# Attention beside a gated MLP on one core: two stages in a hand-set order, scores in 32-row tiles, spatial and output products filled in between

## The chip, the cores and the metric

The kernel runs on one core of one Trainium2 chip. The core has a matrix engine (PE, with weight loads shown as PEld), a vector engine (DVE), a scalar engine (ACT), a general engine (POOL) and a queue engine (SP). Each works through its own instructions in order and waits for the others by semaphores. Matrix products land in PSUM, eight banks of 512 float32 columns on 128 partitions, and are read from there by DVE or ACT. The metric is device microseconds of one execution; lower is better.

## The reference

The input is 2048 tokens of 512 features. One layer norm feeds two branches, and their outputs are added to the input. Branch A is attention with 32 heads of 16 features, in which a token sees itself and the 255 before it. Branch B is a gated MLP: a projection to 2 x 688 features with GELU, a layer norm of the second half, a 2048 x 2048 product over tokens (the spatial product), a gate with the first half, and a product back to 512.

```python
def reference(A_x, A_wqkv, A_wo, B_x, B_w_in, B_w_sp, B_b_sp, B_w_out):
    ...
        scores = jnp.einsum('bhqd,bhkd->bhqk', q, k) * Dh ** (-0.5)
        idx = jnp.arange(S)
        mask = (idx[:, None] - idx[None, :] >= 0) & (idx[:, None] - idx[None, :] < W)
        scores = jnp.where(mask[None, None], scores, -1000000000.0)
        p = _softmax(scores, axis=-1)
        o = jnp.einsum('bhqk,bhkd->bhqd', p, v)
    ...
        z = _gelu(jnp.einsum('bsd,df->bsf', x, w_in))
        z1 = z[..., :Fh].copy()
        z2 = _layernorm(z[..., Fh:], axis=-1)
        g = jnp.einsum('ts,bsf->btf', w_sp, z2) + b_sp[None, :, None]
        return jnp.einsum('bsf,fd->bsd', z1 * g, w_out)
    x = A_x
    xn = _layernorm(x, axis=-1)
    return x + _A_ref(xn, A_wqkv, A_wo) + _B_ref(xn, B_w_in, B_w_sp, B_b_sp, B_w_out)
```

## The kernel before

Tokens are cut into 16 blocks of 128. A start phase loads x, normalizes it (statistics on DVE, an inverse root by 12 small DVE steps for each 4 blocks, L141 to L166), transposes each block on PE (L195) and copies it to xnT on ACT (L198).

Then come 16 steps, one for each block of queries. A step may hold:

- do_z (L206), two blocks in each of the first 8 steps: the projection to 2 x 688 on PE (L214), then GELU by hand. ACT halves the product (L222), DVE makes the argument in three passes (L224 to L229), ACT takes a tanh (L231), DVE finishes (L233, L239) and sums squares (L243).
- do_proj (L270): keys (L275) and queries (L304) by matmuls that move only 128 columns, values (L283) by matmuls that move 512. Queries are made twice, once for the even and once for the odd heads of a pair, with weights whose other half is zero. They are spread over a zeroed tile (qT4, L313 to L317) so that a matmul with all 128 rows picks one pair of heads.
- do_attention (L322): for each of 8 groups of four heads, scores (L341) of two pairs of heads against two or three key blocks, 256 columns each; exp on ACT (L359); triangular masks by DVE (L367, L373) or, in the first 8 steps, one of them by an added matmul (L349); then the product with the values (L382), 17 columns each, the 17th being the sum of the weights. L391 and L393 divide by that sum, and an SP transpose makes oT (L400).
- do_g (L403), from step 8 on: an SP transpose loads a block of w_sp (L406), 32 matmuls make the spatial product (L411), DVE gates it (L417), an SP transpose makes uT (L422).
- do_final (L425): ten matmuls of 512 columns (L432, L438; the last has 48 rows), an add of x by DVE (L443), a store from the ACT queue (L444).

After step 15, eight do_g and do_final are left and run by themselves. All projections and spatial products share one PSUM tile of two banks (gft), scores and outputs have two such tiles (S_t), and the attention result has one (o_t). The order on each engine is made by the framework's scheduler out of the program order and the dependences.

Of the kernel before, what the change touches and what calls it, by code (L numbers as in the profile page):

```python
# [8 lines left out]
P = 128  # L9
BF = mybir.dt.bfloat16  # L10
# [5 lines left out]
D = 512  # L16
H = 32
DH = 16
W = 256
F = 1376  # L20
FH = 688
NQB = S_TOK // P
NDC = D // P
SM_SCALE = DH ** -0.5
GELU_K = 1.5957691216057308
GELU_C = 0.044715
LN_EPS = 1e-5
NG4 = 4
VW = H * 17
UPAD = 768  # L30
NFC = UPAD // P
Z_RANGES = [(0, 512), (512, FH)]
PJ_AHEAD = 1
# [3 lines left out]
def kernel(  # L37
# [18 lines left out]
    eps_t = pers.tile([P, 1], F32, name="eps_t")  # L56
    xnT = pers.tile([P, NDC, S_TOK], BF, name="xnT")
    wq2 = pers.tile([P, NDC, 2, D], BF, name="wq2")
    wk_sb = pers.tile([P, NDC, D], BF, name="wk_sb")
    wv_sb = pers.tile([P, NDC, D], BF, name="wv_sb")  # L60
    wo_sb = pers.tile([P, NDC, D], BF, name="wo_sb")
    w_out_sb = pers.tile([P, NFC, D], BF, name="w_out_sb")
    z1_all = pers.tile([P, NQB, FH], BF, name="z1_all")
    z2n_all = pers.tile([P, NQB, FH], BF, name="z2n_all")
    b_bf = pers.tile([P, NQB], BF, name="b_bf")
    b_all = pers.tile([P, NQB], F32, name="b_all")
    mvx_all = pers.tile([P, NQB, 2], F32, name="mvx_all")
    mv2_all = pers.tile([P, NQB, 2], F32, name="mv2_all")
    rstdx = pers.tile([P, NQB], F32, name="rstdx")
    rstd2 = pers.tile([P, NQB], F32, name="rstd2")  # L70
    sdx = pers.tile([P, NQB], F32, name="sdx")
    sd2 = pers.tile([P, NQB], F32, name="sd2")
    s1_all = pers.tile([P, NQB], F32, name="s1_all")
    s2_all = pers.tile([P, NQB], F32, name="s2_all")
    mean2 = pers.tile([P, NQB], F32, name="mean2")
    var2 = pers.tile([P, NQB], F32, name="var2")
    maskA01 = pers.tile([P, P], BF, name="maskA01")
    maskC01 = pers.tile([P, P], BF, name="maskC01")
    maskAb = pers.tile([P, 2, P], BF, name="maskAb")
    NQRING = 2  # L80
    qT4s = [pers.tile([P, NG4, 4 * 256], BF, name=f"qT4_{i}") for i in range(NQRING)]

    ps_s = ctx.enter_context(tc.tile_pool(name="ps_s", bufs=2, space=bass.MemoryType.PSUM))
    ps_gf = ctx.enter_context(tc.tile_pool(name="ps_gf", bufs=1, space=bass.MemoryType.PSUM))
    ps_o = ctx.enter_context(tc.tile_pool(name="ps_o", bufs=1, space=bass.MemoryType.PSUM))
    xsp = ctx.enter_context(tc.tile_pool(name="xsp", bufs=4))
    bsm = ctx.enter_context(tc.tile_pool(name="bsm", bufs=6))

    XG = 2
    nc.vector.memset(eps_t[:], LN_EPS)  # L90

    make_identity(nc, ident[:])
    nc.vector.memset(maskA01[:], 1.0)
    nc.gpsimd.affine_select(
        out=maskA01[:], in_=maskA01[:], pattern=[[1, P]], compare_op=ALU.is_ge,
        fill=0.0, base=0, channel_multiplier=-1,
    )
    nc.vector.memset(maskAb[:], 0.0)
    nc.gpsimd.affine_select(
        out=maskAb[:], in_=maskAb[:], pattern=[[0, 2], [1, P]], compare_op=ALU.is_ge,  # L100
        fill=-30000.0, base=0, channel_multiplier=-1,
    )
    nc.vector.memset(maskC01[:], 1.0)
    nc.gpsimd.affine_select(
        out=maskC01[:], in_=maskC01[:], pattern=[[-1, P]], compare_op=ALU.is_gt,
        fill=0.0, base=0, channel_multiplier=1,
    )
    nc.vector.memset(wq2[:], 0.0)
    for i in range(NQRING):
        nc.gpsimd.memset(qT4s[i][:], 0.0)  # L110
    nc.gpsimd.dma_start(out=wo_sb[:], in_=A_wo.rearrange("(c p) n -> p c n", p=P))
    nc.gpsimd.dma_start(
        out=w_out_sb[:, 0:5, :], in_=B_w_out[0:640, :].rearrange("(c p) n -> p c n", p=P)
    )
    nc.gpsimd.dma_start(out=w_out_sb[0:48, 5, :], in_=B_w_out[640:688, :])

    with tc.tile_pool(name="wraw_pool", bufs=1) as wrp:
        w_raw = wrp.tile([P, NDC, 3 * D], BF, name="w_raw")
        nc.sync.dma_start(out=w_raw[:], in_=A_wqkv.rearrange("(c p) f -> p c f", p=P))
        for c in range(NDC):  # L120
            sv = w_raw[:, c, 0:D].rearrange("p (G s e j) -> p G s e j", G=NG4, s=4, e=2, j=DH)
            for e in range(2):
                dv = wq2[:, c, e, :].rearrange("p (G s e j) -> p G s e j", G=NG4, s=4, e=2, j=DH)
                nc.vector.tensor_copy(out=dv[:, :, :, e, :], in_=sv[:, :, :, e, :])
            nc.vector.tensor_copy(out=wk_sb[:, c, :], in_=w_raw[:, c, D : 2 * D])
            nc.scalar.copy(out=wv_sb[:, c, :], in_=w_raw[:, c, 2 * D : 3 * D])

    qpool = ctx.enter_context(tc.tile_pool(name="qpool", bufs=2))
    kring = ctx.enter_context(tc.tile_pool(name="kring", bufs=4))
    vring = ctx.enter_context(tc.tile_pool(name="vring", bufs=4))  # L130
    ep = ctx.enter_context(tc.tile_pool(name="ep", bufs=3))
    lpool = ctx.enter_context(tc.tile_pool(name="lpool", bufs=2))
    otpool = ctx.enter_context(tc.tile_pool(name="otpool", bufs=17))
    cpool = ctx.enter_context(tc.tile_pool(name="cpool", bufs=2))
    wsp_pool = ctx.enter_context(tc.tile_pool(name="wsp_pool", bufs=2))

    with ExitStack() as lctx:
        lt = lctx.enter_context(tc.tile_pool(name="lt", bufs=2))
        RS_G = 4

        def rsqrt_batch(n0):  # L141
            sl = slice(n0, n0 + RS_G)
            vpe = bsm.tile([P, RS_G], F32, name="vpe")
            nc.vector.tensor_scalar(
                out=vpe[:], in0=mvx_all[:, sl, 1], scalar1=LN_EPS, scalar2=None, op0=ALU.add
            )
            hx = bsm.tile([P, RS_G], F32, name="hx")
            nc.vector.tensor_scalar(out=hx[:], in0=vpe[:], scalar1=0.5, scalar2=None, op0=ALU.mult)
            yi = bsm.tile([P, RS_G], mybir.dt.int32, name="yi")
            nc.vector.tensor_scalar(  # L150
                out=yi[:], in0=vpe[:].bitcast(mybir.dt.int32), scalar1=1, scalar2=None,
                op0=ALU.arith_shift_right,
            )
            nc.vector.tensor_scalar(
                out=yi[:], in0=yi[:], scalar1=-1, scalar2=0x5F375A86, op0=ALU.mult, op1=ALU.add
            )
            y = yi[:].bitcast(F32)
            ty = bsm.tile([P, RS_G], F32, name="ty")
            for _ in range(3):
                nc.vector.tensor_tensor(out=ty[:], in0=y, in1=y, op=ALU.mult)  # L160
                nc.vector.tensor_tensor(out=ty[:], in0=ty[:], in1=hx[:], op=ALU.mult)
                nc.vector.tensor_scalar(
                    out=ty[:], in0=ty[:], scalar1=-1.0, scalar2=1.5, op0=ALU.mult, op1=ALU.add
                )
                nc.vector.tensor_tensor(out=y, in0=y, in1=ty[:], op=ALU.mult)  # L165
            nc.vector.tensor_copy(out=rstdx[:, sl], in_=y)  # L166

        xs_tiles = {}
        for n in range(NQB):
            tn = n * P  # L170
            if n % RS_G == 0:
                for n2 in range(n // XG, (n + RS_G) // XG):
                    xs = xsp.tile([P, XG, D], BF, name="xs")
                    eng = nc.sync if n2 % 2 == 0 else nc.scalar
                    eng.dma_start(
                        out=xs[:],
                        in_=x2[n2 * XG * P : (n2 + 1) * XG * P, :].rearrange(
                            "(j p) d -> p j d", p=P
                        ),
                    )  # L180
                    for j in range(XG):
                        nn = n2 * XG + j
                        xs_tiles[nn] = xs[:, j, :]
                        stats = bsm.tile([P, nc.vector.BN_STATS_DIM], F32, name="stats")
                        nc.vector.bn_stats(out=stats[:], in_=xs[:, j, :])
                        nc.vector.bn_aggr(out=mvx_all[:, nn, :], in_=stats[:])
                rsqrt_batch(n)
            xn_sb = lt.tile([P, D], BF, name="xn_sb")
            nc.vector.tensor_scalar(  # L189
                out=xn_sb[:], in0=xs_tiles[n], scalar1=mvx_all[:, n, 0:1],  # L190
                scalar2=rstdx[:, n : n + 1], op0=ALU.subtract, op1=ALU.mult,
            )
            tp = ps_s.tile([P, NDC, P], BF, name="tp", tag="S_t")
            for c in range(NDC):
# [253 lines left out]
    for n in range(PJ_AHEAD):  # L448
        do_proj(n)
# [62 lines left out]
```

## Time and profile before

| what | value |
|---|---|
| median of 3 runs | 442.18 us (440.03 to 445.08) |
| the profiled execution, its span | 445.4 us |
| DMA traffic | 24.77 MB, mean 56 GB/s |
| start phase | about 0 to 45 us |
| steps 0 to 7 | about 45 to 218 us |
| steps 8 to 15 | about 218 to 380 us |
| what is left of do_g and do_final | about 380 to 445 us |

"Busy" counts an instruction from its start to its modelled end. PE's instructions overlap, so a group of matmuls costs the time from one start to the next (the pitch), which is less than the duration of one. The chain is followed back from the last instruction to what released each; time on it is time that the span is made of. The granted clock is PE's, 1.00 being full speed.

### The profile page before, as it was taken

How to read it: one execution, taken by the hardware profiler on the slowest of the kernel's cores; microseconds unless marked ns; L12 is line 12 of the kernel's file. 1: busy time of each engine (PE TensorE's matmuls, PEld its weight loads, DVE VectorE, ACT ScalarE, POOL GpSimd, SP SyncE). 2: the span in 40 equal slices, each digit the busy share in tenths (PEclk: the TensorE clock that was granted, in tenths of full speed). 3: DMA queues.
4: the chain of work that ended last, by engine and by line, in shares of the span. 5: the costliest groups of instructions: out<-in, count | busy, mean ns of one | idle time of the engine just before them, and what ended most of it. 6: DMA issues, size and time to landing. Idle time of an engine off the chain costs nothing. (4 is left out here: it accounts for less than half of the span.)

```text
span 445.4 us, 9799 instructions
## 1 busy us (share of the span) xinstructions
PE 373.5 (84%) x4112; PEld 253.2 (57%) x4112; DVE 284.8 (64%) x682; ACT 240.8 (54%) x344; POOL 25.2 (6%) x62
## 2 busy tenths in 40 slices
PE   0126678899998989898799989898989899999996
PEld 0114355667675757676576656665666667455552
DVE  4919488887979797979965665656565654412222
ACT  3112565696878787979665728374645559100000
POOL 9100000000000000000000000000000000011010
PEclk9975999999999999999989999999999999999999
DMA  8990300000001000000003050604040323566551
GB/s 242 114 179 24 128 1 13 1 13 1 13 1 14 2 13 1 13 8 7 1 13 79 1 102 1 102 1 102 4 100 17 87 38 66 118 161 146 121 130 42
DMA packets 63548, 24.77 MB, mean 56 GB/s; under 512 B 57568, under 2 KB 61664, under 8 KB 63504
## 3 DMA queue, kind: packets, MB, share of 16 engines
q1 hardware_dynamic: 58464, 16.26, 19.7%
q10 hardware_dynamic: 3920, 4.56, 3.3%
q0 software_dynamic: 1120, 3.33, 3.3%
q8 instruction: 32, 0.52, 0.5%
q14 instruction: 12, 0.10, 0.1%
HBM read 8.41 MB, written 2.10 MB: 24 GB/s over the span
## 5 line engine op out<-in xcount | busy, mean ns | idle before, releaser
L359 ACT ACTIVATE E_t<-S_t 128x768 bf16<-128x768 f32 (+2 forms) x256 | 183.9, 769 | 83.5 <-PE S_t L341 47.6
L411 PE MATMUL gft<-z2n_all,wspT 128*128 128x512 bf16 (+1 forms) x512 | 93.9, 309 | 2.4 <-DVE qtmp L313 2.3
L341 PEld LDWEIGHTS <-kT 128*128 128x128 bf16 x720 | 64.1, 97 | 42.9 <-issue 27.8
L341 PE MATMUL S_t<-qT_0_83,kT 128*128 128x256 bf16 x352 | 59.4, 273 | 9.7 <-ACT E_t L359 6.2
L341 PE MATMUL S_t<-qT_1_84,kT 128*128 128x256 bf16 x368 | 60.1, 271 | 8.6 <-ACT E_t L359 7.2
L382 PEld LDWEIGHTS <-E_t 128*128 128x128 bf16 x1440 | 48.5, 96 | 29.5 <-DVE E_t L373 15.0
L382 PE MATMUL o_t<-v_t,E_t 128*128 128x17 bf16 x1440 | 56.8, 171 | 5.0 <-ACT E_t L359 2.8
L411 PEld LDWEIGHTS <-wspT 128*128 128x128 bf16 x512 | 45.3, 97 | 22.6 <-issue 2.0
L367 DVE TENSOR_TENSOR E_t<-E_t,maskA_80 128x512 bf16<-128x512 bf16 x64 | 27.2, 425 | 44.4 <-ACT E_t L359 44.1
L373 DVE TENSOR_TENSOR E_t<-E_t,maskC_81 128x512 bf16<-128x512 bf16 x112 | 46.5, 419 | 12.5 <-ACT E_t L359 12.3
L214 PE MATMUL gft<-w_in_sb,xnT 128*128 128x512 bf16 (+1 forms) x256 | 45.7, 308 | 6.3 <-DMA w_in_sb<-in_B_w_in_dram 2.1
L304 PEld LDWEIGHTS <-wq_61 128*128 128x128 bf16 x512 | 31.7, 102 | 11.7 <-DVE v_t L295 5.9
L304 PE MATMUL gft<-xnT,wq_61 128*128 128x128 bf16 x512 | 34.1, 226 | 4.4 <-DVE yi L165 3.8
L417 DVE SCALAR_TENSOR_TENSOR u_sb<-gft,b_all,z_all 128x688 bf16<-128x688 f32 x16 | 14.2, 890 | 33.1 <-PE gft L411 29.0
L349 PE MATMUL S_t<-maskAb,ident 128*128 128x256 bf16 x128 | 33.8, 272 | 0.0
L214 PEld LDWEIGHTS <-xnT 128*128 128x128 bf16 x256 | 22.3, 97 | 19.5 <-issue 8.5
L195 PE MATMUL tp<-ident,xn_sb 128*128 128x128 bf16 x64 | 8.4, 285 | 29.7 <-DVE xn_sb L189 29.2
L222 ACT ACTIVATE zb<-gft 128x688 bf16<-128x688 f32 x32 | 23.8, 745 | 13.1 <-PE gft L214 11.1
L231 ACT ACTIVATE th<-wt 128x688 bf16<-128x688 bf16 x32 | 24.8, 776 | 6.4 <-DVE wt L229 5.2
L438 PE MATMUL S_t<-w_out_sb,uT 128*128 128x512 bf16 x96 | 25.2, 380 | 0.7 <-DMA uT<-u_sb 0.7
L313 DVE CAST qtmp<-gft 128x1024 bf16<-128x1024 f32 x16 | 19.6, 1223 | 7.5 <-PE gft L304 7.4
L195 PEld LDWEIGHTS <-xn_sb 128*128 128x128 bf16 x64 | 6.3, 130 | 31.2 <-DVE xn_sb L189 30.2
(71 smaller groups left out, 349.1 us busy)
## 6 DMA issues: line engine op xcount, KB each, us to landing
x_ch<-in_A_x_dram POOLq DMA_DIRECT2D x16, 128.0 KB, 3.3
out_dram<-out_sb ACTq DMA_DIRECT2D x16, 128.0 KB, 2.4
w_raw<-in_A_wqkv_dram SPq DMA_DIRECT2D x1, 1536.0 KB, 7.9
w_in_sb<-in_B_w_in_dram ACTq DMA_DIRECT2D x1, 1376.0 KB, 5.8
xs<-in_A_x_dram ACTq DMA_DIRECT2D x4, 256.0 KB, 6.9
xs<-in_A_x_dram SPq DMA_DIRECT2D x4, 256.0 KB, 6.7
w_out_sb<-in_B_w_out_dram POOLq DMA_DIRECT2D x1, 640.0 KB, 16.2
wo_sb<-in_A_wo_dram POOLq DMA_DIRECT2D x1, 512.0 KB, 6.6
```

The lines of the kernel that those rows point to most:

```text
L214: nc.tensor.matmul(zp[:, lo:hi], lhsT=xnT[:, c, tn : tn + P], rhs=w_in_sb[:, c, f0 + lo : f0 + hi], start=(c == 0), stop=(c == NDC - 1),)
L222: nc.scalar.mul(out=zb[:], in_=zp[:, 0:FH], mul=0.5)
L231: nc.scalar.activation(out=th[:], in_=wt[:], func=ACT.Tanh, scale=GELU_K)
L304: nc.tensor.matmul(qpf[:, col0 : col0 + P], lhsT=wq2[:, c, e, G * P : (G + 1) * P], rhs=xnT[:, c, tn : tn + P], start=(c == 0), stop=(c == ...
L341: nc.tensor.matmul(S_tiles[sp][:, 256 * b : 256 * b + 256], lhsT=kTb[:, G, :], rhs=qT[:, G, 256 * s : 256 * s + 256], start=True, stop=not ...
L349: nc.tensor.matmul(S_tiles[sp][:, 512:768], lhsT=ident[:], rhs=maskAb[:].rearrange("p e c -> p (e c)"), start=False, stop=True,)
L359: nc.scalar.activation(out=dste[:, :, b_lo:3, :], in_=src[:, :, b_lo:3, :], func=ACT.Exp, scale=SM_SCALE,)
L367: nc.vector.tensor_tensor(out=regA, in0=regA, in1=maskA01[:].unsqueeze(1).to_broadcast([P, 4, P]), op=ALU.mult,)
L373: nc.vector.tensor_tensor(out=regC, in0=regC, in1=maskC01[:].unsqueeze(1).to_broadcast([P, 4, P]), op=ALU.mult,)
L382: nc.tensor.matmul(o_t[:, bank, 17 * hh : 17 * hh + 17], lhsT=E_t[:, j, 128 * b : 128 * b + 128], rhs=v_tiles[kb][:, 17 * h : 17 * h + 17] ...
L411: nc.tensor.matmul(gf[:, lo:hi], lhsT=wspT[:, c, :], rhs=z2n_all[:, c, lo:hi], start=(c == 0), stop=(c == NQB - 1),)
L438: nc.tensor.matmul(fo, lhsT=uT[0:K, ch, :], rhs=w_out_sb[0:K, ch, :], start=False, stop=(ch == NFC - 1),)
```

## The change

The whole body is rewritten, and the order on each engine is now the order in which the program is written.

Stage 1 makes everything that comes from xnT. x is loaded in seven pieces on the queues of SP and ACT with the weights of do_z in between; the weights of the outputs move from POOL's queue to SP's, behind x. The inverse root is one power on POOL. z_half makes half a projection block and applies GELU in a single ACT instruction; the second layer norm uses bn_stats. qkv_unit makes queries or keys for 128 features and 512 tokens by four matmuls of 512 columns, or values of a block of 128 tokens by four of 512. Queries are made once and copied twice with a mask for even and odd heads (one copy on DVE, one on ACT). 39 of the 48 such units run between the halves of blocks 3 to 15.

Stage 2 is 184 sets. A set takes two pairs of heads, in two row tiles of 32 rows, against 1024 columns of scores in all, followed by one exp of 1024 columns (kinds BC, AB, CA: which key block meets which of two query blocks; 512 columns for one kind in the first two blocks). After the scores of a set come the masks that are due on DVE (one set late), up to 9 matmuls with the values (three sets late), and filler: the 9 units left, spatial products in two halves of 344 columns, and outputs, 1447 columns a set. What is left of the filler runs at the end. PSUM is cut anew: two tiles of two banks for scores, two of one bank for attention results, two of one bank for filler. The store of the result moves from ACT's queue to POOL's.

```diff
+    ctx.enter_context(tc.manual_schedule())
...
     ps_s = ctx.enter_context(tc.tile_pool(name="ps_s", bufs=2, space=bass.MemoryType.PSUM))
+    ps_o = ctx.enter_context(tc.tile_pool(name="ps_o", bufs=2, space=bass.MemoryType.PSUM))
+    ps_f = ctx.enter_context(tc.tile_pool(name="ps_f", bufs=2, space=bass.MemoryType.PSUM))
...
+    def qkv_unit(b, i):
+        t0 = b * 512
+        pt = bank()
+        if i < 8:
+            G, isk = divmod(i, 2)
+            w0 = isk * D + G * P
+            for c in range(NC):
+                nc.tensor.matmul(
+                    pt[:], lhsT=wqkv[:, c, w0 : w0 + P], rhs=xnT[:, c, t0 : t0 + 512],
+                    start=(c == 0), stop=(c == NC - 1),
+                )
+                yield 512
+            if isk:
+                nc.scalar.copy(out=kT[:, G, t0 : t0 + 512], in_=pt[:])
+            else:
+                nc.vector.tensor_scalar(
+                    out=qpad[:, G, 0, t0 : t0 + 512], in0=pt[:],
+                    scalar1=hmask[:, 0:1], scalar2=None, op0=ALU.mult,
+                )
+                nc.scalar.mul(out=qpad[:, G, 1, t0 : t0 + 512], in_=pt[:], mul=hmask[:, 1:2])
...
+        load_x(nc.sync, 0, 1)
+        load_x(nc.scalar, 1, 2)
+        load_x(nc.sync, 2, 3)
+        load_x(nc.scalar, 3, 4)
+        nc.sync.dma_start(out=w_in_sb[:, :, 0:FH], in_=w_in_v[:, :, 0:FH])
+        nc.scalar.dma_start(out=w_in_sb[:, :, FH:F], in_=w_in_v[:, :, FH:F])
+        load_x(nc.sync, 4, 8)
+        nc.sync.dma_start(out=wqkv[:], in_=A_wqkv.rearrange("(c p) f -> p c f", p=P))
+        load_x(nc.sync, 8, 12)
+        load_x(nc.sync, 12, 16)
...
+            nc.gpsimd.tensor_tensor(
+                out=rs[:, 0:k], in0=ve[:, 0:k], in1=mhalf[:, 0:k], op=ALU.pow
+            )
...
+        def z_half(n, half):
+            zp = ps_s.tile([P, 2, 512], F32, name="zp", tag="S")
+            for c in range(NC):
+                for j in range(2):
+                    f0 = half * FH + j * HALF
+                    nc.tensor.matmul(
+                        zp[:, j, 0:HALF],
+                        lhsT=xnT[:, c, n * P : (n + 1) * P],
+                        rhs=w_in_sb[:, c, f0 : f0 + HALF],
+                        start=(c == 0), stop=(c == NC - 1),
+                    )
+            dst = (z1 if half == 0 else z2n)[:, n, :]
+            nc.scalar.activation(
+                out=dst.rearrange("p (j f) -> p j f", j=2),
+                in_=zp[:, :, 0:HALF], func=ACT.Gelu_apprx_tanh,
+            )
...
+            z_half(n, 0)
...
+            if n >= 3:
+                for _ in qkv_unit(*qkv_list.pop(0)):
+                    pass
+            z_half(n, 1)
...
+    def g_unit(t):
+        u = cp.tile([P, UPAD], BF, name="u")
...
+        uT = cp.tile([P, NFC, P], BF, name="uT", bufs=4)
+        nc.sync.dma_start_transpose(out=uT[:], in_=u[:])
+        uTs[t] = uT
+        u_ready[t] = clock[0] + DMA_STEPS
+        if t + 2 < NB:
+            load_wsp(t + 2)
...
+        def pick(self, drain):
+            if self.qkv:
+                return qkv_unit(*self.qkv.pop(0))
+            if self.fq:
+                t = self.fq[0]
+                if t in u_ready and t in o_ready and (
+                    drain or clock[0] >= max(u_ready[t], o_ready[t])
+                ):
+                    self.fq.pop(0)
+                    return f_unit(t)
+            if self.gq:
+                return g_unit(self.gq.pop(0))
+            return None
...
+    def do_scores(J, G, kind, sp):
...
+        for kb, qs, nq, col in segs:
+            for i in range(2):
+                s = 2 * sp + i
+                nc.tensor.matmul(
+                    S[:, i, col : col + 2 * nq],
+                    lhsT=kT[32 * s : 32 * s + 32, G, kb * P : (kb + 1) * P],
+                    rhs=qpad[32 * s : 32 * s + 32, G, :, qs : qs + nq],
+                    start=True, stop=True,
+                )
+        nc.scalar.activation(
+            out=Et[:, 2 * sp : 2 * sp + 2, c0:512], in_=S[:, :, c0:512],
+            func=ACT.Exp, scale=SM_SCALE,
+        )
...
+    PV_RATE = 9
+    total_fill = 9 * 2048 + NB * 32 * HALF + (NB - 2) * (NC + NFC) * 512
+    per_set = total_fill / len(sets)
+    i = 0
+    while i < len(sets) or mask_q or pv_q or pv_cur is not None:
+        clock[0] = i
+        if i < len(sets):
+            J, G, kind, sp, last = sets[i]
+            do_scores(J, G, kind, sp)
+        while mask_q and mask_q[0][0] <= i:
+            do_masks(*mask_q.pop(0)[1])
+        if i < len(sets):
+            if sp == 1:
+                mask_q.append((i + 1, (J, G, kind)))
+            if last:
+                pv_q.append((i + 3, (J, G)))
+        n = 0
+        while n < PV_RATE:
+            if pv_cur is None:
+                if not pv_q or pv_q[0][0] > i:
+                    break
+                pv_cur = pv_unit(*pv_q.pop(0)[1])
+            if next(pv_cur, 0):
+                n += 1
+            else:
+                pv_cur = None
+        if i < len(sets):
+            fill.pull(per_set)
+        i += 1
+    while fill.step(True):
+        pass
```

More of the change, by code (lines that the diff above doesn't have):

```diff
@@ L72 @@
[L72 to L81, printed above, removed]
@@ L94 @@
[L94 to L107, printed above, removed]
@@ L108 @@
[L108 to L126, printed above, removed]
@@ L154, in rsqrt_batch, with z_apply @@
+        def z_apply(n, rs):
             nc.vector.tensor_scalar(
[L155 to L165 removed]
@@ L166, in rsqrt_batch @@
[L166 to L191, printed above, removed]
-            )
-            tp = ps_s.tile([P, NDC, P], BF, name="tp", tag="S_t")
-            for c in range(NDC):
-                nc.tensor.transpose(
-                    out=tp[:, c, :], in_=xn_sb[:, c * P : (c + 1) * P], identity=ident[:]
-                )
-            nc.scalar.copy(out=xnT[:, :, tn : tn + P], in_=tp[:, :, :])
@@ L425, in do_final @@
[L425 to L435 removed]
+                out=z2n[:, n, :], in0=z2n[:, n, :],
+                scalar1=zmv[n // 2][:, n % 2, 0:1], scalar2=rs[:, n % 2 : n % 2 + 1],
```

654 lines of the change are left out of this document (331 added, 323 removed).

## The prediction, on record before the result

> **What bounds the kernel now.** I read the page's busy shares first, then busy time in four stretches (windows), then the chain of waits, and last single runs of instructions in the timeline, for pitches.
>
> ```profile
> PE 373.5 (84%) x4112; PEld 253.2 (57%) x4112; DVE 284.8 (64%) x682; ACT 240.8 (54%) x344; POOL 25.2 (6%) x62
> ...
> 0.00:45.00 45.00, 11.71 (x95) 9.57 (x96) 27.84 (x134) 9.65 (x17) 12.54 (x22) 0.81 0.77 138
> 45.00:218.00 173.00, 150.03 (x1817) 108.06 (x1815) 142.48 (x313) 133.97 (x199) 1.18 (x5) 1.00 0.06 15
> 218.00:380.00 162.00, 150.73 (x1839) 104.57 (x1839) 98.43 (x216) 97.22 (x130) 6.04 (x20) 0.99 0.25 49
> 380.00:446.00 66.00, 61.00 (x367) 30.97 (x364) 16.02 (x22) 0.00 (x0) 5.45 (x15) 0.99 0.52 121
> ```
>
> In each window row the columns are the stretch, its length, busy PE, PEld, DVE, ACT and POOL, the granted clock and the DMA figures. PE is the busiest engine everywhere except in the first 45 us, where it does almost nothing. Busy says how many instructions are in flight, not what they cost, so I price PE by pitch. These rows give it:
>
> ```profile
> 44.71 0.23 PE L195 MATMUL tp<-ident,xn_sb 128*128 128x128 bf16 x1
> ...
> 45.00 0.39 PE L195 MATMUL tp<-ident,xn_sb 128*128 128x128 bf16 x4
> ...
> 265.39 0.45 PE L382 MATMUL o_t<-v_t,E_t 128*128 128x17 bf16 x12
> 265.70 0.71 PE L341 MATMUL S_t<-qT_0_83,kT 128*128 128x256 bf16 x5
> ...
> L341 PE MATMUL S_t<-qT_0_83,kT 128*128 128x256 bf16 x352 | 59.4, 273 | 9.7 <-ACT E_t L359 6.2
> L382 PEld LDWEIGHTS <-E_t 128*128 128x128 bf16 x1440 | 48.5, 96 | 29.5 <-DVE E_t L373 15.0
> L382 PE MATMUL o_t<-v_t,E_t 128*128 128x17 bf16 x1440 | 56.8, 171 | 5.0 <-ACT E_t L359 2.8
> ...
> 260.13 1.00 PE gft L275 x16
> 261.13 0.86 PE gft L283 x4
> 263.77 1.80 PE gft L304 x32
> 265.59 1.24 DVE qtmp L313
> 281.29 1.00 PE gft L275 x16
> 389.22 4.77 PE gft L411 x32
> 393.99 0.86 PE S_t L432 x4
> 394.86 1.40 PE S_t L438 x6
> 396.25 4.77 PE gft L411 x32
> ```
>
> A run lasts (n-1) pitches and one duration. 17 columns: (0.45 - 0.171)/11 = 0.025 us. 256 columns: (0.71 - 0.273)/4 = 0.11. On the chain the runs follow each other, so 512 columns cost 0.86/4 = 0.215, and 128 columns 1.80/32 = 0.056 (a transpose is as cheap: four in 0.39, one lasting 0.23). The 32 matmuls of L411 cost 4.77, of which 0.10 is the way out of the 48-row matmul (below): 4.67/16 = 0.292 for 688 columns, 0.146 for 344.
>
> PE's necessary work by these pitches: transposes 64 x 0.056 = 3.6; do_z 128 pairs x 0.292 = 37.4; do_proj 16 x 3.66 = 58.6; scores 720 x 0.11 = 79; mask matmuls (L349) 128 x 0.11 = 14; values 1440 x 0.025 = 36; spatial 16 x 4.67 = 74.7; outputs 16 x (2.26 + 0.10) = 37.8. Sum 341 of 445.4 us. So 104 us are lost. Where: about 40 in the start phase; some 3 in each step (from one L275 row to the next 21.16 us pass, and the work in it is 3.66 + 48 x 0.11 + 96 x 0.025 + 4.77 + 2.26 = 18.4), of which 1.24 is PE waiting for DVE to empty the only gft tile; the rest while do_z shares that tile with do_proj; and 6 us at the end. From 45 to 218 us DVE is busy 142 of 173 us too, so removing PE work alone would help little there.
>
> **The change part by part.**
>
> Start. x comes in pieces of 128 KB ahead of the big weights. The nearest rows:
>
> ```profile
> x_ch<-in_A_x_dram POOLq DMA_DIRECT2D x16, 128.0 KB, 3.3
> w_in_sb<-in_B_w_in_dram ACTq DMA_DIRECT2D x1, 1376.0 KB, 5.8
> ...
> 40.07 1.89 PE L304 MATMUL gft<-xnT,wq_61 128*128 128x128 bf16 x16 [3.81 <-DVE yi L165]
> ...
> L185 DVE BATCH_NORM_STATS2 stats<-xs 128x6 f32<-128x512 bf16 x16 | 10.5, 670 | 9.4 <-DMA xs<-in_A_x_dram 9.4
> ```
>
> Issue at 0.8, landing 3.3 later, four statistics at 0.67 with their aggregation, the root, one normalization, four transposes and a copy: the first z matmul at about 9 us; w_in, issued behind x (5.8 from issue to landing before), should be there by then. Ends: 8 and 14. At 40 us 16 matmuls of 128 columns took 1.89, a pitch of 0.11 for 0.056: PE starts at half speed. I add 3 us for that.
>
> Stage 1 empties PSUM with instructions like these:
>
> ```profile
> L222 ACT ACTIVATE zb<-gft 128x688 bf16<-128x688 f32 x32 | 23.8, 745 | 13.1 <-PE gft L214 11.1 <-PE S_t L349 1.3 <-DVE z_all L233 0.2
> L198 ACT COPY xnT<-tp 128x512 bf16<-128x512 bf16 x16 | 8.9, 587 | 27.9 <-PE tp L195 27.9
> L393 DVE TENSOR_TENSOR o_norm<-o_t,rsum 128x512 bf16<-128x512 f32 x16 | 10.9, 680 | 0.1
> ```
>
> On PE stage 1 has transposes 3.6, z 32 x 8 x 0.146 = 37.4, 39 units of four 512-column matmuls at 0.86 = 33.5; sum 74.5. All 48 units cost 41.3 against do_proj's 58.6: the zero half of the queries is no longer streamed. GELU by hand goes (six long instructions a half, of which ACT and DVE did 32 each), and one ACT instruction of the size of L222 stays. What is left for ACT is 32 x 0.75 + 16 x 0.59 + 26 x 0.59 = 49 us and for DVE about 62 (statistics like L185, 26 evacuations like L393, normalizations), both under 74.5, so they lie beside PE. Their waits do not all: in a fixed order, a transpose that wants a PSUM tile waits until an evacuation of 0.7 us is through its queue. I take 5 us for that (ends 0 and 15).
>
> The power on POOL replaces 12 small DVE steps a batch; no row shows it. Beyond the start it has a block's time to run, so I take nothing.
>
> Between the stages: a table load and the first exp, 2 us.
>
> Stage 2. Its new element is a matmul with 32 rows. The nearest thing in this trace is the last matmul of do_final, with 48 rows, between neighbours with 128:
>
> ```profile
> 395.56 0.38 PE L438 MATMUL S_t<-w_out_sb,uT 128*128 128x512 bf16 x1
> 395.87 0.39 PE L438 MATMUL S_t<-w_out_sb,uT 48*128 48x512 bf16 x1
> 396.19 0.39 PE L411 MATMUL gft<-z2n_all,wspT 128*128 128x512 bf16 x1
> ```
>
> The starts are 0.31 and 0.32 apart instead of 0.215: 0.10 us to go in, 0.10 to come out, though both sides were ready. Every set has scores with 32 rows and then values and filler with 128, so I charge each set 0.20. Ends: nothing (a 32-row tile may be prepared while the array works), and 0.52. For the upper end, a matmul that lasts 0.38 is followed after 0.215, so 0.165 of it is draining; a switch that waits for all of it and then for a weight load of 0.096 (PEld L382, above) costs 0.26. I take the row itself.
>
> Beside this stands a rule. The Trainium skill, "TensorEngine Tiling (Array Packing)", section "Key Properties", says that changing the tiling mode drains the engine. The 48-row rows agree in kind. By a full drain the sum below would be 59 us longer; the rows show less than half of it.
>
> Scores: two row tiles work on different heads, each 512 columns a set. If they run at the same time, 0.215 a set, and I add 0.03 for the second one's weights (a pitch of 0.025 in L382 is a weight load and a matmul): 0.25. If one waits for the other, 0.43. No run here shows two tiles at once. The Trainium skill, "TensorE: Matmul & The Clock Gate", "Part 3: Packing small matmuls", says tiles in different row groups run concurrently and gives 3.07 times for four; by that two would be near what I take.
>
> Values: 1440 matmuls over 184 sets, 7.83 x 0.025 = 0.20. Filler: 9 units 7.8, spatial 74.7, 14 outputs of 2.36 = 33.0 (their 48-row switch included); 115.5/184 = 0.63. A set costs PE 0.25 + 0.20 + 0.20 + 0.63 = 1.28, and 184 sets 235 us.
>
> Does another engine need more?
>
> ```profile
> 266.39 3.69 ACT L359 ACTIVATE E_t<-S_t 128x768 bf16<-128x768 f32 x5 [2.24 <-PE S_t L341]
> ...
> L359 ACT ACTIVATE E_t<-S_t 128x768 bf16<-128x768 f32 x224 | 169.4, 810 | 78.2 <-PE S_t L341 47.6 <-PE S_t L349 13.2 <-issue 10.4
> L373 DVE TENSOR_TENSOR E_t<-E_t,maskC_81 128x512 bf16<-128x512 bf16 x112 | 46.5, 419 | 12.5 <-ACT E_t L359 12.3
> L224 DVE TENSOR_TENSOR wt<-zb 128x688 bf16<-128x688 bf16 x32 | 16.5, 515 | 10.4 <-ACT zb L222 10.2
> L417 DVE SCALAR_TENSOR_TENSOR u_sb<-gft,b_all,z_all 128x688 bf16<-128x688 f32 x16 | 14.2, 890 | 33.1 <-PE gft L411 29.0 <-issue 4.1
> L391 DVE RECIPROCAL rsum<-o_t 128x32 f32<-128x32 f32 x16 | 5.7, 355 | 6.8 <-PE o_t L382 6.8
> L359 ACT ACTIVATE E_t<-S_t 128x512 bf16<-128x512 f32 x16 | 8.8, 594 | 2.8 <-PE S_t L349 2.7
> ```
>
> Five exps of 768 columns took 3.69, a pitch of 0.72; 0.84 ns a column (810 against 594 for 256 less) makes 0.94 for 1024. That is under 1.28 and hides; were a set cheaper than 0.94 on PE, ACT would hold it at 173 us. Masks: 0.55 ns a column from 419 and 515 gives 0.70 for 1024 and 1.26 for 2048 columns, 80 us in all; with gating 17 (32 halves of L417 at 0.53), 16 output adds of L393's size 11, and 32 norms of about 0.96 (L391, and L393's 0.68 in two pieces of 0.30), DVE has 139 of 235. A mask is done about 0.9 us before its value matmuls come up; that slack is also what the queues may eat. On POOL the store now stands before the next x_ch, and waits for DVE's add; x_ch lands 3.3 after its issue while an output takes 3.5 sets, so an add may wait half a microsecond, with masks behind it, inside the slack. The output weights now stand behind x on SP's queue; their first user comes 30 sets into stage 2. On SP each uT transpose waits for its gate, with the next w_sp load behind it, and both have some 7 sets.
>
> PE still meets unfinished work at times. Before, 2.8 of 21.16 us a step was lost, 13%, with one tile where there are now two; I take 4% or 9.4 us (ends 0 and 31).
>
> Tail. A transpose by SP takes:
>
> ```profile
> oT<-o_norm SPq DMA_TRANSPOSE x16, 3.1
> out_dram<-out_sb ACTq DMA_DIRECT2D x16, 128.0 KB, 2.4
> ```
>
> After the last scores come exp, the largest mask, 48 value matmuls, norm, this transpose, 14 output matmuls, the add and the store: 1.6 past the last set, then 1.2, 1.2, 3.1, 3.2, 0.7 and 3.5 us (2.4 and its issue by POOL); together 14.5 (ends 11 and 18).
>
> Sum: 9 + 3 + 74.5 + 5 + 2 + 235 + 9.4 + 14.5 = 352 us of span. The profiled span of before, 445.4, stands to its median, 442.18, as 1 to 0.993; so 350 us. PE's work falls only from 341 to 314 (queries 17 less, mask matmuls 14 less, scores 33 less, switches 37 more); the other 65 us are waiting that goes.
>
> **The rivals.**
>
> The tiles do not overlap: the row tiling then does not do what it says, since the columns streamed are the same as before. 0.18 x 184 = 33 us more, 384. For: nothing here shows overlap. Against: different rows and different banks.
>
> The switch drains in full: 0.32 x 184 = 59 more, 409. Against: three rows with 0.10.
>
> The switch hides: 0.20 x 184 = 37 less, 313. For: weights of 32 rows might load early. Against: both directions show it.
>
> The hand-set order loses as much as the steps before, 13% of 235 = 31 instead of 9: 372. For: PE takes no other ready work. Against: double tiles.
>
> Slower than before: the round trip of a set is far dearer with 32 rows than with 48. It would need 0.20 + 92/184 = 0.70 us a set to reach 442. Against: that is three and a half times what the 48-row rows show.
>
> **How the numbers follow.** The forecast, 350 with its own range 335 to 366, gets 0.50; no overlap 0.15; order losses 0.12; hidden switch 0.10; full drain 0.08; the dear switch 0.04; 0.01 for the rest. 315 to 392 holds the first three and about half of the hidden switch, 0.82. Changes under 1% can't be told from none. Faster by over 1% holds all but the dear switch and the rest: 0.95; within 1% 0.01; slower 0.04.
>
> **What would show it.** Score matmuls of a pair starting within 0.05 us: overlap; 0.2 apart: none. The first scores and the first value matmul of a set each 0.1 late: the switch. First z matmul near 9 us, stage 2 starting near 94, a set pitch near 1.3, PE busy to the last set, and a tail of about 15. Wrong would be a set pitch above 1.5, long waits of PE for exp or masks, or ACT without gaps.

## The result, and the profile after

The changed kernel takes 337.85 us (median of 4 runs, 337.48 to 338.79) against 443.63 us for the kernel before beside it: a ratio of 0.764, interval 0.760 to 0.769. The forecast was 350 us.

Below are the page's busy shares and the head of its chain, below them the same head and the first piece of the chain for the kernel before, then busy time by stage (the columns as in the prediction: stretch and length, PE, PEld, DVE, ACT, POOL, granted clock, DMA). The stages are cut at the first z matmul, the first and the last scores.

```profile
PE 312.3 (93%) x3079; PEld 154.9 (46%) x3104; DVE 195.6 (58%) x397; ACT 236.4 (70%) x267; POOL 34.5 (10%) x76
...
PE 88%; DMA 3%; DVE 3%; ACT 2%; issue 2%; POOL 0%; SPq 0%; POOLq 0%; ACTq 0%
```

```profile
PE 38%; issue 2%; DVE 2%; ACT 1%; DMA 1%; ACTq 0%; DVEq 0%; SPq 0%
...
244.86 2.02 issue
```

```profile
0.00:8.95 8.95, 1.03 (x8) 0.82 (x9) 5.33 (x16) 2.17 (x4) 3.04 (x9) 1.00 0.81 273
8.95:88.72 79.77, 76.95 (x461) 44.54 (x470) 55.49 (x132) 45.75 (x73) 11.38 (x19) 1.00 0.23 63
88.72:318.00 229.28, 225.92 (x2522) 105.62 (x2537) 130.21 (x240) 187.48 (x190) 17.41 (x44) 1.00 0.36 71
318.00:335.80 17.80, 8.40 (x94) 3.93 (x91) 4.61 (x10) 1.02 (x1) 2.71 (x5) 0.78 0.20 55
```

The chain is now 88% PE. The 38% of before can't be set against it: that chain could be followed back only to 244.86 us, and its shares add up to less than half of the span. What compares is PE's busy share, 84% before and 93% now. In stage 2 ACT has 187 and DVE 130 of 229 us: both have room, and PE has none. What PE does in a set shows in the timeline (start, length, engine, line, operation):

```profile
200.62 0.31 PE L348 MATMUL gf<-z2n,wspT 128*128 128x344 bf16 x1
200.86 0.39 PE L460 MATMUL S<-qpad,kT 32*128 32x512 bf16 x2
201.18 0.38 PE L503 MATMUL o<-v_all,E 128*128 128x17 bf16 x9
201.42 0.74 PE L348 MATMUL gf<-z2n,wspT 128*128 128x344 bf16 x4
202.10 0.39 PE L460 MATMUL S<-qpad,kT 32*128 32x512 bf16 x2
```

Two score matmuls of 512 columns are over in 0.39 us, the duration of one: they start 3 to 4 ns apart, so the row tiles overlap fully. From the last 344-column matmul to the first score 0.24 us pass in place of 0.145, and from the scores to the values 0.32 in place of 0.215. That is the switch, 0.10 in and 0.10 out, as at the 48-row matmul of before. One set takes 201.18 - 200.86 = 0.32, then 0.24 for nine value matmuls and 0.68 for four filler matmuls with the way in: 1.24 us.

### The profile page after: what moved, and what is told of

The parts are those of the page before. It is cut to its first block, busy times and chain, and to the rows that moved or that the text cites. A ratio compares the mean times of both kernels' runs of the same rounds, so it can differ in the third digit from the quotient of the medians.

```text
span 335.8 us, 7241 instructions
## 1 busy us (share of the span) xinstructions
PE 312.3 (93%) x3079; PEld 154.9 (46%) x3104; DVE 195.6 (58%) x397; ACT 236.4 (70%) x267; POOL 34.5 (10%) x76
## 4 chain that ended last, share of the span: by engine, by line
PE 88%; DMA 3%; DVE 3%; ACT 2%; issue 2%; POOL 0%; SPq 0%; POOLq 0%; ACTq 0%
PE gf L348 23%; PE S L460 17%; PE o L503 15%; PE zp L234 11%; PE fo L374 6%; PE fo L380 4%; PE pj_f L93 4%; PE pj_o L93 4%; DMA w_in_sb<-in_B_w_in_dram 2%; PE pj_o L109 2%; PE pj_f L109 2%; DVE qpad L101 1%; ACT qpad L105 1%; DMA oT<-on_4384 1%; ACT E L467 1%
## 5 line engine op out<-in xcount | busy, mean ns | idle before, releaser
L467 ACT ACTIVATE E<-S 128x1024 bf16<-128x1024 f32 (+1 forms) x184 | 184.5, 1007 | 40.8 <-PE S L460 38.6
L348 PE MATMUL gf<-z2n,wspT 128*128 128x344 bf16 x512 | 95.2, 308 | 0.0
L460 PE MATMUL S<-qpad,kT 32*128 32x512 bf16 (+1 forms) x480 | 70.7, 329 | 2.4 <-ACT E L467 2.2
L503 PEld LDWEIGHTS <-E 128*128 128x128 bf16 x1440 | 47.7, 96 | 39.5 <-issue 32.2
L503 PE MATMUL o<-v_all,E 128*128 128x17 bf16 x1440 | 64.0, 172 | 1.7 <-DVE E L483 1.6
L483 DVE TENSOR_TENSOR E<-E,maskCA 128x2048 bf16<-128x2048 bf16 (+1 forms) x32 | 37.0, 1157 | 33.2 <-ACT E L467 33.2
L234 PE MATMUL zp<-w_in_sb,xnT 128*128 128x344 bf16 x256 | 43.9, 319 | 0.3 <-DMA w_in_sb<-in_B_w_in_dram 0.3
L483 DVE TENSOR_TENSOR E<-E,maskA 128x1024 bf16<-128x1024 bf16 x32 | 22.1, 690 | 32.7 <-ACT E L467 32.7
L374 PE MATMUL fo<-w_out_sb,uT 128*128 128x512 bf16 (+1 forms) x81 | 26.9, 392 | 1.0 <-issue 0.2
L483 DVE TENSOR_TENSOR E<-E,maskC 128x1024 bf16<-128x1024 bf16 x28 | 19.3, 689 | 3.8 <-ACT E L467 1.7
```

What stands on the lines that cost most here:

```text
L234: nc.tensor.matmul(zp[:, j, 0:HALF], lhsT=xnT[:, c, n * P : (n + 1) * P], rhs=w_in_sb[:, c, f0 : f0 + HALF], start=(c == 0), stop=(c == NC ...
L348: nc.tensor.matmul(gf[:, 0:HALF], lhsT=wspT[t][:, c, :], rhs=z2n[:, c, j * HALF : (j + 1) * HALF], start=(c == 0), stop=(c == NB - 1),)
L374: nc.tensor.matmul(fo[:], lhsT=uTs[t][0:K, ch, :], rhs=w_out_sb[0:K, ch, :], start=(ch == 0), stop=False,)
L460: nc.tensor.matmul(S[:, i, col : col + 2 * nq], lhsT=kT[32 * s : 32 * s + 32, G, kb * P : (kb + 1) * P], rhs=qpad[32 * s : 32 * s + 32, G, ...
L467: nc.scalar.activation(out=Et[:, 2 * sp : 2 * sp + 2, c0:512], in_=S[:, :, c0:512], func=ACT.Exp, scale=SM_SCALE,)
L483: nc.vector.tensor_tensor(out=ap, in0=ap, in1=m.unsqueeze(1).to_broadcast([P, ap.shape[1], ap.shape[2]]), op=ALU.mult,)
```

## The experiments

Each is a change of the changed kernel, except where it says so. Times are medians in us.

**One row tile.** Both score matmuls of a set read the rows of the first head pair.

```diff
-                s = 2 * sp + i
+                s = 2 * sp
```

> Both score matmuls of a set use the rows of the first head pair, so the second head pair's scores are not computed; columns, exps and everything else stay. In the changed kernel the two start 2 to 4 ns apart. Theory (PE sets the pace of a set, and the two row tiles overlap): they now follow each other, 0.215 us more in each of 184 sets (half of that in 8 of them), so 337.9 + 39 = 377 us. Rival (ACT's exp of 0.92 to 1.02 us sets the pace, and score time hides beside it): 338 to 342 us.

Measured: 375.5. In its timeline:

```profile
200.04 0.74 PE L348 MATMUL gf<-z2n,wspT 128*128 128x344 bf16 x4
200.72 0.60 PE L460 MATMUL S<-qpad,kT 32*128 32x512 bf16 x2
201.25 0.38 PE L503 MATMUL o<-v_all,E 128*128 128x17 bf16 x9
```

The pair now takes 0.60 instead of 0.39, and 184 x 0.21 is the 38 us. So the overlap is worth 38 us, and PE, not ACT, sets the pace of a set.

**Scores apart.** One row tile before the values, the other behind them.

```diff
+            do_scores(J, G, kind, sp, 0)
...
+            do_scores(J, G, kind, sp, 1)
             fill.pull(per_set)
```

> The two row tiles of a set are issued apart: one before the matmuls with the values, one behind them, so a set goes into the 32-row matmuls and out of them twice; everything is computed as in the changed kernel. Theory (0.2 us for each round trip, and the overlap of the two tiles lost, which by the run with one row tile is worth 37.7 us): 337.9 + 37.7 + about 175 sets with values x 0.2 = 410 us. Rival (the round trip costs nothing of its own, only the loss of overlap counts): 376 us.

Measured: 408.6, 33 us over the run with one row tile: 0.19 us for each of some 175 more round trips. Its timeline:

```profile
201.09 0.38 PE L463 MATMUL S<-qpad,kT 32*128 32x512 bf16 x1
201.40 0.39 PE L508 MATMUL o<-v_all,E 128*128 128x17 bf16 x9
201.72 0.39 PE L463 MATMUL S<-qpad,kT 32*128 32x512 bf16 x1
202.04 0.76 PE L348 MATMUL gf<-z2n,wspT 128*128 128x344 bf16 x4
```

Scores to values, values to scores and scores to filler are each 0.31 to 0.32 apart, where 512 columns cost 0.215 and nine value matmuls 0.24 without a switch behind them. The switch is paid in full in the kernel's time, and does not hide.

**48 rows padded to 128.** Zeros in the output weights.

```diff
+        nc.gpsimd.memset(w_out_sb[:, 5, :], 0.0)
...
-            K = P if ch < NFC - 1 else FH - (NFC - 1) * P
+            K = P
```

> The last 48 rows of the output weights are padded with zeros to 128, so that the 48-row matmul of each output has 128 rows; the columns streamed are the same. Theory (0.10 us in and 0.10 out for each change of the row tiling): 16 x 0.2 = 3.2 us less, 334.7 us. Rival (the 0.10 on either side of that matmul belongs to the place, not to the change of rows): 337.9 us, no change.

Measured: 336.4 (335.4 to 337.7), which overlaps the 337.5 to 338.8 of the changed kernel a little: the total alone doesn't decide between the two. The trace does. The first pair of rows below is from the changed kernel's timeline, the second from the padded one's:

```profile
317.02 0.39 PE L374 MATMUL fo<-w_out_sb,uT 48*128 48x512 bf16 x1
...
317.34 0.61 PE L380 MATMUL fo<-wo_sb,oT 128*128 128x512 bf16 x2
```

```profile
316.55 0.38 PE L375 MATMUL fo<-w_out_sb,uT 128*128 128x512 bf16 x1
316.77 0.59 PE L381 MATMUL fo<-wo_sb,oT 128*128 128x512 bf16 x2
```

0.32 has become 0.22, and from first to last scores 227.0 us pass instead of 229.3. The rest is covered by the start, where the first z matmul varies between 8.95 and 10.8 us from one profiled run to another.

**Scores of two sets together.**

```diff
-            do_scores(J, G, kind, sp)
+            if i % 2 == 0:
+                do_scores(*sets[i][:4])
+                do_scores(*sets[i + 1][:4])
...
-        while n < PV_RATE:
+        while n < 2 * PV_RATE:
...
-            fill.pull(per_set)
+            fill.pull(2 * per_set)
```

> The scores of two sets are issued back to back, then the masks, the matmuls with the values and the filler of both. Theory (each way in and out of the 32-row matmuls costs 0.2 us together, and head pairs in different rows overlap): half of the round trips go, 92 x 0.2 = 18 us, and four tiles at once take the time of two, 92 x 0.215 = 20 us more; but with two score tiles in PSUM the second half of the scores waits for the exp of the set before, which I put at 0.19 us of a pair: 314 us, with ACT nearly without gaps. Rival (the price is not in the switch but in draining what stands before, or the wait for the score tiles takes all back): 333 us or more.

Measured: 322.2, between the two. Its busy time by stage, from the first scores on:

```profile
88.80:298.30 209.50, 203.75 (x2510) 109.01 (x2525) 127.29 (x240) 176.90 (x189) 16.58 (x43) 0.99 0.39 76
298.30:319.60 21.30, 11.97 (x110) 4.95 (x103) 5.15 (x11) 1.94 (x2) 3.60 (x7) 0.70 0.20 56
```

Stage 2 fell by 20 us. The terms of the expectation say as much: 18 + 20 - 92 x 0.19 = 21, which makes 317 and not the 314 that it names. The end grew by 3.5: two adds there stand 3.3 us each for x_ch, where the changed kernel has one. From the first scores of a pair to the first values 0.52 us pass on average, 0.20 more than for one set, where 0.19 was put. A pair of this run shows why:

```profile
203.98 1.02 ACT L467 ACTIVATE E<-S 128x1024 bf16<-128x1024 f32 x1
...
204.75 0.69 PE L460 MATMUL S<-qpad,kT 32*128 32x512 bf16 x4
205.05 0.09 PEld L460 LDWEIGHTS <-kT 32*128 32x128 bf16 x1 [0.21 <-issue]
```

The exp that reads the other score tile ends at 205.00, and the last weights go in at 205.05: four matmuls take 0.69 instead of 0.39. So 92 round trips are saved, and part of the overlap of four is not had with two score tiles.

**Filler behind the attention.** Only the nine projection units stay in between. (All sixteen oT are kept then, in xnT's place.)

```diff
+    fill.gq = []
+    fill.fq = []
...
-    while fill.step(True):
-        pass
+    for t in range(NB + 1):
+        if t < NB:
+            for _ in g_unit(t):
+                pass
+        if t > 0:
+            for _ in f_unit(t - 1):
+                pass
```

> Only the nine projection units are filled in between; spatial and output matmuls come after the attention, one spatial block ahead of each output, with the same instructions. Theory (the filler is what PE does while ACT works on exp): attention alone is set by ACT, 184 x 0.94 = 173 us, and the filler adds 16 x 4.67 + 16 x 2.36 = 112 us behind it, so 89 + 173 + 5 + 112 + 8 = 387 us. Rival (the gain comes from the work removed and the projections ahead, the order of the filler matters little): under 350 us.

Measured: 388.3. Busy time in stage 1, in the attention and in what follows:

```profile
10.40:90.30 79.90, 77.08 (x460) 44.51 (x467) 54.07 (x132) 45.33 (x72) 9.87 (x17) 1.00 0.22 58
90.30:262.00 171.70, 163.79 (x1886) 79.69 (x1887) 101.43 (x195) 169.06 (x190) 1.72 (x4) 0.56 0.06 13
262.00:386.00 124.00, 115.62 (x734) 66.45 (x741) 32.57 (x56) 1.55 (x2) 18.26 (x45) 0.97 0.55 120
```

Its exps as a group, and two sets of its timeline:

```profile
L469 ACT ACTIVATE E<-S 128x1024 bf16<-128x1024 f32 x176 | 162.3, 1125 | 0.7 <-PE S L462 0.5
...
149.94 0.61 PE L462 MATMUL S<-qpad,kT 32*128 32x512 bf16 x2
150.48 0.41 PE L505 MATMUL o<-v_all,E 128*128 128x17 bf16 x9
150.86 0.61 PE L462 MATMUL S<-qpad,kT 32*128 32x256 bf16 x4
```

ACT is busy 169 of 171.7 us of attention and stood only 0.7 us in all before 176 exps: without filler it is the bound, at the 173 us worked out from exp's pitch. PE looks busy there too, but at a granted clock of 0.56 on average. Scores and nine value matmuls take it 0.92 (150.86 - 149.94), the pace of ACT's exps, where they took 0.56 in the changed kernel: busy time alone would mislead. What brings the clock down no run isolates. The filler is worth 50 us.

**Narrow operands.**

```diff
+            for m in range(4):
...
-                    pt[:], lhsT=wqkv[:, c, w0 : w0 + P], rhs=xnT[:, c, t0 : t0 + 512],
+                        pt[:, m * P : (m + 1) * P], lhsT=wqkv[:, c, w0 : w0 + P],
+                        rhs=xnT[:, c, t0 + m * P : t0 + (m + 1) * P],
```

> The query and key units move 128 columns in each matmul, 16 matmuls in place of 4; what is computed is the same, queries still once. Theory (a pitch of 0.056 us for 128 columns against 0.215 for 512: width is worth nearly nothing, what the change saved was the zero half of the queries): 32 units x (16 x 0.056 - 4 x 0.215) = 1 us, 338.5 to 340 us. Rival (wide operands are what made the projections cheap, because a weight load stands before each matmul): 32 x 12 x 0.04 or more, above 350 us.

Measured: 340.1 (337.7 to 340.5), 2 us over the changed kernel, of which stage 1 has 0.7 (80.5 against 79.8) and the rest lies in the start and the end. So width is worth about 2 us at most. Of the 17 us that the prediction has for the projections, the larger part is then the zero half that is no longer streamed, some 14 by its pitches (16 x 0.9); no run streams it again.

**GELU by hand.** The six instructions of before in place of one.

```diff
-                in_=zp[:, :, 0:HALF], func=ACT.Gelu_apprx_tanh,
+            nc.scalar.mul(
...
+            nc.scalar.activation(out=th[:], in_=wt[:], func=ACT.Tanh, scale=1.5957691216057308)
```

> GELU is again made by hand: ACT halves the product, DVE makes three passes, ACT takes tanh, DVE finishes; statistics stay as changed. Theory (beside wide projections DVE bounds stage 1 as it did together with PE before): DVE's 55 us of stage 1 grow by 32 x 2.2 = 70 to about 126, so stage 1 takes 126 to 135 instead of 80 us and the kernel 384 to 393 us. Rival (these passes hide beside PE, the single instruction only relieves idle engines): 338 to 345 us.

Measured: 442.3. Both expectations failed: the loss is 104 us, not 50. Below, two rows of the waits (us in total, times, longest), and the busy time of stage 1:

```profile
ACT th L253 <- DVE wt L251: 74.0, 32, 4.6
ACT qpad L105 <- DVE qpad L101: 37.2, 15, 4.5
...
10.20:185.50 175.30, 103.43 (x460) 52.40 (x467) 116.43 (x248) 64.25 (x99) 10.66 (x19) 0.77 0.10 28
```

DVE has 116 of 175 us, so it isn't the bound; in the order written, ACT stands at each tanh until DVE has made its argument, with its evacuations for PE queued behind. The next run takes the same instructions in another order, and the one after it also moves ACT's query copies to DVE.

**Tanh one half later.**

```diff
+            z_tail()
...
+            late.append((dst, zb, wt))
```

> GELU by hand as in the run before (442 us, where ACT waited 74 us for DVE's argument), but the tanh and what follows it are issued one half block later, behind the next half's first ACT instruction. The instructions are the same. Theory A (the cost was the hand-set order: each queue stands still while the chain ACT, DVE, ACT, DVE of one half runs, and PE's clock falls with it): stage 1 falls to DVE's own work, 126 to 135 us instead of 178, and the kernel to 385 to 400 us. Theory B (DVE and ACT simply have that much work, in any order): 430 us or more.

Measured: 424.8. Better, but between the theories: ACT now waited 60 us at its copy of the queries for DVE's copy of the same PSUM tile.

**And both query copies on DVE.**

```diff
-                nc.scalar.mul(out=qpad[:, G, 1, t0 : t0 + 512], in_=pt[:], mul=hmask[:, 1:2])
+                nc.vector.tensor_scalar(
+                    out=qpad[:, G, 1, t0 : t0 + 512], in0=pt[:],
```

> GELU by hand with the late tanh (425 us), and both masked copies of the queries on DVE. In the run before this one ACT waited 60 us at its copy of the queries for DVE's copy of the same PSUM tile. Theory (what stage 1 lost beyond DVE's work is this wait between two queues, with ACT's evacuations behind it): DVE's work in stage 1 is 126 + 11 us, so stage 1 falls from 155 to 138 to 145 us and the kernel to 405 to 415 us. Rival (DVE itself is what lasts, and 11 us more on it add up): 430 to 436 us.

Measured: 399.0, under the range expected, with 12 us of copies more on DVE. Busy time of stage 1:

```profile
10.49:143.29 132.80, 91.45 (x468) 48.79 (x468) 119.25 (x258) 57.98 (x88) 11.90 (x18) 0.83 0.13 36
```

DVE is now busy 119 of 133 us, where the expectation had 137 of work, and comes near to bounding stage 1. Of the 104 us that GELU by hand cost, 43 were the order and the split of the copies between the two queues. The other 61 are what it still costs in the best of the three orders: 53 in stage 1, 7 in stage 2, the rest in the start. That all of it is work is not shown, since DVE still stands 14 us.

**GELU in one instruction in the kernel before,** its scheduler and order unchanged.

```diff
-                zb = zt.tile([P, FH], BF, name="zb")
-                nc.scalar.mul(out=zb[:], in_=zp[:, 0:FH], mul=0.5)
...
+                dst = (z1_all if half == 0 else z2n_all)[:, n, :]
+                nc.scalar.activation(out=dst, in_=zp[:, 0:FH], func=ACT.Gelu_apprx_tanh)
```

> The kernel before with one part of the change alone: GELU in a single ACT instruction and the second layer norm's statistics by bn_stats; its scheduler, tiles and order stay. Theory (in steps 0 to 7 of before, PE and DVE were both nearly full and the rest was waiting on single PSUM tiles, so taking 70 us of DVE work away lets PE fill some of its 25 us of gaps there, less 2 x 1.3 us a step for exchanging the tables of GELU and exp): 420 to 440 us. Rival (GELU by hand was worth the 87 to 104 us that it costs in the hand-set order): 335 to 355 us.

Measured: 496.0, ratio 1.125 (1.119 to 1.130) to the kernel before. Both expectations failed, in sign too. Two groups of its instructions, and a piece of ACT's timeline:

```profile
L336 ACT ACT_TABLE_LOAD x33 | 42.3, 1283 | 0.6
L222 ACT ACT_TABLE_LOAD x32 | 41.1, 1283 | 0.6
...
102.03 1.28 ACT L222 ACT_TABLE_LOAD   x1
103.33 0.74 ACT L222 ACTIVATE z2n_all<-gft 128x688 bf16<-128x688 f32 x1
104.09 1.28 ACT L336 ACT_TABLE_LOAD   x1
```

The scheduler weaves each GELU between exps, and each change between the two loads a table: 65 loads of 1.28, 83 us of ACT, where I had counted two a step. The kernel before, with tanh between the same exps, has three loads in all, and the changed kernel has two. The Trainium skill, "ScalarE: Activation LUTs", section "Table sets: the hidden batching unit", says to batch calls by set; these rows agree. So in the order of before the single GELU loses, and the change can use it because it takes exp out of the stage that holds it. Whether gathering the GELUs of each step in the kernel before would do as well was not run.

**Together.** Scores of two sets, padded rows, and x_ch loaded one output earlier.

```diff
-        x_ch = cp.tile([P, D], BF, name="x_ch")
-        nc.gpsimd.dma_start(out=x_ch[:], in_=x2[t * P : (t + 1) * P, :])
+        for m in range(t, min(t + 2, NB)):
+            if m not in x_chs:
+                x_chs[m] = cp.tile([P, D], BF, name="x_ch", bufs=3)
+                nc.gpsimd.dma_start(out=x_chs[m][:], in_=x2[m * P : (m + 1) * P, :])
+        x_ch = x_chs[t]
```

> Scores of two sets back to back, as in the run that took 322 us, the 48-row matmul padded to 128, and each x_ch loaded one output earlier, since at the end DVE stood 3.3 us before an add with the last mask behind it. Theory: 3 us for the rows, of which part is lost where the scores wait for exp, and 2 to 4 us in the last stretch: 316 us. Rival (with two sets together the score tiles set the pace, and the end is bound by the transposes): 321 to 323 us.

Measured: 315.4 (315.2 to 315.7): 2.3 us less in stage 2 and 4.5 less at the end, against scores of two sets alone. Then both query copies on DVE as well:

> The version that took 315.4 us, with both masked copies of the queries on DVE, so that ACT no longer waits there (15 us of ACT's idle time in stage 1). Theory (PE's short stalls in stage 1 hang on that wait): stage 1 falls by 2 to 4 us, 312 to 314 us. Rival (DVE has 55 of 80 us there, and its longer queue holds the other evacuations back): 315.4 us or more.

Measured: 311.8 (311.3 to 314.1), the fastest, 0.707 of the kernel before (0.703 to 0.710) and 26 us under the changed one. Stage 1 fell from 79.5 to 77.9 us, less than was expected, and stage 2 from 207.2 to 205.1, which was not expected, so the total is right in part by luck. PE's first wait for an exp, in the run before and in this one, shows the second:

```profile
93.52 0.28 PE L464 MATMUL S<-qpad,kT 32*128 32x256 bf16 x2 [2.17 <-ACT E L471]
```

```profile
90.58 0.28 PE L467 MATMUL S<-qpad,kT 32*128 32x256 bf16 x2 [0.42 <-ACT E L474]
```

Where no query copy stands ahead of the first exp in ACT's queue, that exp begins 1.1 us after the first scores instead of 2.9, and PE waits 0.42 instead of 2.17.

## Why the prediction held, point by point

**The start** was put at 9 us, and the first z matmul came at 8.95. Eight other runs had 9.8 to 10.8: there it waited 1.1 to 2.0 us for w_in, which the prediction had in place by then, and here 0.3. So part of that agreement is luck.

**Stage 1** was put at 3 + 74.5 + 5 + 2 = 84.5 us and took 79.8. The pitches held; the allowances for a cold clock, for evacuations and for the change of stage were too large together by 4.7. The named mechanism is there (ACT's copy of the queries waits 15 us in all for DVE's, with xnT's copy behind it), but it costs PE little: PE stands 2.8 of the 79.8 us.

**GELU** was costed at nothing because one ACT instruction lies beside PE. That is right for the changed kernel (ACT 46, DVE 55 of 80 us). What the text didn't see is on what it hangs: by hand it costs 61 us more even in the best order run, and the single instruction alone in the old order makes the kernel 54 us slower.

**The switch** was put at 0.20 a set from a 48-row matmul. It is 0.20 by the pitches and 0.19 by the run with scores apart. The Trainium skill, "TensorEngine Tiling (Array Packing)", section "Key Properties", has the engine drain at a change of mode. That there is a price agrees; it is less than half of the 0.26 each way that draining a whole matmul and then loading weights would take.

**Overlap** was put at 0.25 for the scores of a set, 0.03 of it for the second tile's weights. It is 0.22: the second starts 4 ns after the first. With 184 sets these 0.03 are 5.5 us of the miss.

**Waiting in stage 2** was put at 4%, 9.4 us, from the steps of before. PE stood 3.4 us there (225.92 busy of 229.28). Two rows of the waits (who waited for whom, us in total, times, longest), and the longest of the first row in the timeline:

```profile
PE S L460 <- ACT E L467: 2.2, 2, 1.8
...
PE o L503 <- DVE E L483: 1.6, 1, 1.6
...
92.69 0.28 PE L460 MATMUL S<-qpad,kT 32*128 32x256 bf16 x2 [1.75 <-ACT E L467]
```

In all of the kernel PE waited 2.2 us for exp and 1.6 for a mask, and 1.75 of the 2.2 is the change of stage, for which the prediction had 2 us of its own. So this term was 6 us too large, about as much as the overlap and the allowances of stage 1. The 48 value matmuls of the tail stand in the prediction twice, in stage 2 and in the tail, which is 1.2 us more. Stage 2 with its last set took 230.5 (229.3 and 1.2) where 244.4 stood.

**The end** was put at 14.5 past the last set, 1.2 us after the last scores began; it took 16.6. PE runs at half speed for a while, and DVE stands before the last add until x_ch lands:

```profile
322.62 2.23 PE L374 MATMUL fo<-w_out_sb,uT 128*128 128x512 bf16 x5 [0.23 <-issue]
...
325.54 1.04 PE L380 MATMUL fo<-wo_sb,oT 128*128 128x512 bf16 x4 [0.69 <-DMA oT<-on_4384]
...
327.91 1.04 PE L380 MATMUL fo<-wo_sb,oT 128*128 128x512 bf16 x4
...
330.67 0.69 DVE L386 TENSOR_TENSOR ot<-fo,x_ch 128x512 bf16<-128x512 f32 x1 [3.36 <-DMA x_ch<-in_A_x_dram]
```

Five matmuls take 2.23 instead of 1.24, but that cost nothing: behind them PE still waits 0.69 for oT. The last add has its product at 328.95 and starts at 330.67, so the wait for x_ch, which POOL could issue only behind the store before it, costs 1.7 us. Loading x_ch earlier, with the padding, took 4.5 us off the end of the run with the scores of two sets, which stood at 21.3; against the 17.8 of the changed kernel it is 1.0.

**The sum.** 352 of span stood against 335.8: stage 1 was 4.7 us shorter, stage 2 with its last set 13.9 shorter, the end 2.1 longer. The factor of 0.993 to the median went the wrong way: the profiled execution of before was a long one, and here a run's time is 1.7 us above its own span (337.5 for 335.8).

**The rivals.** No overlap was put at 33 us more, and taking the overlap away cost 38. The hidden switch and the full drain are excluded by the two rows of pitches, the dear switch too. The loss in the hand-set order did not appear here, but it is real: the same kernel with GELU by hand lost 43 us to it, in stage 1.

**What stays open.** The prediction has 65 us of waiting go. No run keeps the order and takes the second PSUM tiles away, or the other way round, so how the two share in it is not shown. The start, about 45 us before and 9 now, is about a third of the gain, and no run takes its parts (x ahead of the big weights, the root on POOL) one by one.

## What to carry to other kernels

Price a matrix engine by pitch, row by row, and look for a rare instruction in the trace that stands for the new one: a single 48-row matmul gave the price of 184 switches. A fixed order is as good as its queues: it lost almost nothing where each engine's next instruction was ready in time, and 43 us where two engines handed one tile back and forth. Before a fused function replaces several, look at which functions alternate with it on ACT.

## What the runs showed of the hardware that was not expected

An exchange of GELU's and exp's tables costs 1.3 us each time: a load of 1.28, and the next instruction 0.02 behind it (102.03 and 103.33 above).

Two row tiles overlap fully (one duration, 0.39 us, for two matmuls of 512 columns), and going into 32 rows and out costs 0.10 us each, the same as for 48 rows.

PE's granted clock was 0.56 in the attention without filler, 0.77 in stage 1 with GELU by hand, and 0.78 in the last 18 us of the changed kernel, against 1.00 where PE had work all the time (stages 1 and 2 of the changed kernel). How much standing still it takes, these runs don't show.
